# Performer attention, a merged expert layer and a routed expert layer: the place of the output's zeros, the queue of batch 1's stores, the engine of half the expert low parts, and the banks of the second kv half

## Chip, cores and metric

The kernel runs on one core of a Trainium2 chip. The metric is the device time of one execution in microseconds. Before the change the median of three runs is 358.18 us (357.52 to 359.08).

## What is computed

Three layers follow one another; all inputs and the output are float32.

```python
# 1. attention with random features, q and k: 2 batches x 8 heads x 576 tokens x 64
def phi(x):
    proj = np.einsum('bhsd,md->bhsm', x, omega)          # 128 features
    h = proj - np.sum(x * x, axis=-1, keepdims=True) / 2.0
    return np.exp(h - np.max(h, axis=-1, keepdims=True)) / np.sqrt(m)
q_p, k_p = phi(q * scale), phi(k * scale)
kv = np.einsum('bhsm,bhsd->bhmd', k_p, v)
num = np.einsum('bhsm,bhmd->bhsd', q_p, kv)
den = np.einsum('bhsm,bhm->bhs', q_p, np.sum(k_p, axis=2))[..., None] + 1e-06
x = num / den                                            # as 1152 tokens x 512
# 2. w1, w2: 512 x 1024, w3: 1024 x 1024, w_out: 1024 x 512
x = ((x @ w1) * (x @ w2) @ w3) @ w_out
# 3. 8 experts, each with 288 slots; a token goes to the expert of its largest logit
logits = x @ w_gate                                      # softmax of the chosen one: gate_w
h = np.maximum(np.einsum('ecd,edf->ecf', disp, e1), 0.0) # 512 -> 1024
y = np.einsum('ecf,efd->ecd', h, e2)                     # 1024 -> 512
out[i] = gate_w[i] * y[expert_idx[i], pos[i]]            # 0 for a token without a slot
```

## The kernel before

**Precision.** A float32 operand is split in a high part (a cast, on ScalarE) and a low part (operand less high part), and a product is made of three TensorE products: high by high, low by high, high by low. So each weight that arrives by DMA goes through a conversion before TensorE can use it. The weights w1, w2, w3 and w_out arrive as pairs of 32 bit words: VectorE puts the words together (lines 325 to 327 early, in `to_f32_task` later), ScalarE casts, and GpSimd subtracts (line 364). Expert weights arrive as float32: ScalarE casts (line 750) and VectorE subtracts (line 754), in two halves of 512 columns per piece.

**Stages.** First the features of k and q, in 18 units of 128 tokens (`phi_g`), the sums kv over the tokens of batch 0 and of batch 1 (`kv_add`; the accumulators are opened in PSUM by `kv_open`, closed by a copy to `kvz`), and the attention output x. PSUM has eight banks in three pools: `pa` with four, `pm` with two and `px` with two. Batch 0's kv lies in the two `pm` banks, batch 1's in the two `px` banks, which the projection of the features uses too. `KV_AT` names behind which unit which products of kv run.

Then a middle stage. It computes g = (x w1) * (x w2), transposed, in eight column blocks of 128 (f = 0 to 7) and four token chunks of 288 (`ab_mm`, line 433: 12 products of 128x288 each), and beside it W[f], the f-th 128 rows of w3 w_out (24 products of 128x512, line 472). W[f] is copied twice from PSUM by ScalarE and its low part is made on GpSimd (line 480). Its transpose (`u` pieces, line 492) and the product of that with w_gate (`v` pieces, line 500) lead to the logits, which are thus computed from g (`l` and `h` pieces, line 505), without x W.

Then routing and the expert stage. Each of the two batches has 576 tokens. g is transposed on VectorE and stored to a table in DRAM, `gd`, by `to_tokens`: for each batch two halves of four column blocks, and each half by four DMAs (line 410), on ScalarE's queue for the first half and SyncE's for the second. `route` finds expert and slot of each token (lines from 640 on), `gather` builds indices (`r_oh`, line 783) and fetches 288 rows by indirect DMA on GpSimd (line 806), `to_features` transposes them (`r_pt`), `product` multiplies by W (`r_x2p`, 96 products, with a high and a low part, x2, line 837), `hidden` by the expert's first matrix (`r_hp`, line 855) and `result_t` by its second (`r_yt`, line 893). `scatter` writes the rows to the output, which `zeroed` (lines 567 to 573) has filled with zeros by one DMA of 2304 KB. Round r0 holds the tokens of batch 0 for the expert most in demand at the head of the queue of experts, r1 those of batch 1; if more rounds were needed a loop at the end would run them.

**What sets the order.** TensorE's order is the order in which the program is written, and that is set by two strings: `PLAN` (middle stage) and `END` (rest). In `PLAN` a word is a piece: `aFB` the products of column block F for batch B, `WF` the products of W[F], `eFC` one token chunk, `uF`, `vF`, `lF`, `hF` as above, `cF` and `tF` the request for w1/w2 block F and for w3 block F, `z` the zeros. A request is put in a list (`push`); its load is issued on SyncE's queue as soon as one of the two buffers of its ring is free (`pump`). The stages of a conversion are issued one at a time by `tick()`, which the pieces call at their ends, and `need()` issues what is still missing. In `END` a letter is a step of a generator: `p` and `P` a part of `product` of r0 and r1, `h`/`H` of `hidden`, `s`/`S` of `result_t`, `t`/`T` of `to_features`, `K` and `R` logits and routing of batch 1, `F` its gather, `A` a block of g, and `.` is a `tick()`. `w`, `x` and `y` request expert weights; the letter `e` allows conversions of expert weights to begin. From the mark `|` in `PLAN` on, the order of ScalarE, VectorE, GpSimd and SyncE is fixed too, as it is emitted (`keep_order`): an instruction that waits holds all behind it on its engine.

The functions that the change touches:

## Time and profile before

| | us |
|---|---|
| median of three runs | 358.18 |
| lowest, highest | 357.52, 359.08 |
| the profiled execution | 358.03 |
| its span, first to last instruction | 356.1 |
| TensorE busy in the span | 332.1 |
| VectorE, ScalarE, GpSimd busy | 222.4, 146.8, 111.8 |

The profiled execution has its own time, 358.03 us; the span of its instructions is 1.9 us shorter, and all positions below are microseconds from the start of the span. The mean granted TensorE clock over the span is 0.972 of full speed. An engine's busy time says how much it worked; what it waited for is in brackets behind a row of the time line, with the idle time and the operation that ended it.

### The profile page before, as it was taken

What the parts mean: (1) busy time and instruction counts of PE and PEld (TensorE: products, weight loads), DVE (VectorE), ACT (ScalarE), POOL (GpSimd) and SP (SyncE); (2) the same over time, 40 slices, a digit from 0 to 9 for tenths busy, and PEclk for the clock granted to TensorE, in tenths of its full rate; (3) what the DMA queues carried; (4) which work ended last, traced back from release to release, by engine and by line L of the source; (5) the groups of instructions that cost most, each with busy time, mean ns of one, the idle gap of its engine ahead of it and who ended that gap; (6) DMA issues with size and microseconds to landing.
All of it is one profiled execution on the core that took longest, in us unless ns stands there. A gap on an engine that the chain in (4) does not pass through costs nothing. (4 is left out here: it accounts for less than half of the span.)

```text
span 356.1 us, 7072 instructions
## 1 busy us (share of the span) xinstructions
PE 332.1 (93%) x2771; PEld 306.5 (86%) x2771; DVE 222.4 (62%) x442; ACT 146.8 (41%) x347; POOL 111.8 (31%) x102
## 2 busy tenths in 40 slices
PE   7999799999998999989999959999996899999991
PEld 6899799999997988968898938899795799999991
DVE  4989999998997449455959230462764744743110
ACT  4998898634222432423343221222724145442100
POOL 4738610224352424634756521014000120120021
PEclk9999999999999999999999976999997899999998
DMA  7984202235457379923343630468595291510001
GB/s 262 395 311 149 62 2 61 61 120 140 159 151 259 123 109 204 244 65 118 115 124 120 249 135 2 86 49 245 166 183 147 82 291 56 202 44 2 1 24 50
DMA packets 25147, 47.76 MB, mean 134 GB/s; under 512 B 3116, under 2 KB 12460, under 8 KB 25110
## 3 DMA queue, kind: packets, MB, share of 16 engines
q1 hardware_dynamic: 19318, 41.36, 39.7%
q10 hardware_dynamic: 4736, 2.36, 4.1%
q0 software_dynamic: 1056, 3.54, 3.7%
q8 instruction: 24, 0.39, 0.5%
q14 instruction: 13, 0.11, 0.1%
HBM read 38.98 MB, written 8.27 MB: 133 GB/s over the span
## 5 line engine op out<-in xcount | busy, mean ns | idle before, releaser
L433 PE MATMUL ab<-xh,w_hl 128*128 128x288 f32 x512 | 110.4, 304 | 6.0 <-POOL w_hl L364 2.7
L433 PEld LDWEIGHTS ab<-xh,w_hl 128*128 128x128 f32 x512 | 85.4, 192 | 8.6 <-POOL w_hl L364 3.0
L433 PE MATMUL ab<-xl,w_hl 128*128 128x288 f32 x256 | 76.7, 300 | 0.0
L433 PEld LDWEIGHTS ab<-xl,w_hl 128*128 128x128 f32 x256 | 49.3, 193 | 0.0
L472 PE MATMUL W<-wo_hl,w_hl 128*128 128x512 f32 x192 | 46.6, 397 | 1.2 <-POOL w_hl L364 1.2
L472 PEld LDWEIGHTS W<-wo_hl,w_hl 128*128 128x128 f32 x192 | 35.4, 188 | 10.2 <-POOL w_hl L364 1.6
L364 POOL TENSOR_TENSOR w_hl<-w_f,w_hl 128x512 fp32r<-128x512 f32 x22 | 30.6, 1400 | 4.0 <-ACT w_hl L360 4.0
L405 DVE STREAM_TRANSPOSE gs<-g 128x576 f32<-128x576 f32 x16 | 19.6, 1223 | 18.8 <-POOL g L446 18.6
L350 DVE TENSOR_SCALAR w_f<-w_raw 128x512 uint32<-128x512 uint32 x22 | 15.0, 680 | 21.7 <-POOL w_hl L364 16.8
L834 PE MATMUL r_x2p<-r_xc,W 128*128 128x288 f32 x192 | 26.8, 298 | 0.2 <-DVE r_xc L823 0.2
L360 ACT CAST w_hl<-w_f 128x512 fp32r<-128x512 f32 x22 | 13.7, 624 | 31.3 <-DVE w_f L355 31.1
L834 PEld LDWEIGHTS r_x2p<-r_xc,W 128*128 128x128 f32 x192 | 25.8, 188 | 0.6 <-DVE r_xc L823 0.4
L437 ACT COPY a_sb<-ab 128x288 f32<-128x288 f32 x32 | 12.7, 398 | 29.3 <-PE ab L433 29.3
L869 POOL DMA_INDIRECT out<-r_yo,r_odx x6 | 6.1, 1024 | 57.7 <-DVE r_yo L868 48.7
L480 POOL TENSOR_TENSOR W<-W_raw,W 128x512 fp32r<-128x512 f32 x8 | 10.6, 1322 | 43.1 <-ACT u_all L501 27.7
L331 POOL TENSOR_TENSOR wo_hl<-wo_f,wo_hl 128x512 fp32r<-128x512 f32 x8 | 11.2, 1402 | 33.3 <-PE xT L276 16.9
L331 POOL TENSOR_TENSOR w_hl<-w_f,w_hl 128x512 fp32r<-128x512 f32 x10 | 14.2, 1418 | 22.5 <-ACT w_hl L330 19.9
L355 DVE SCALAR_TENSOR_TENSOR w_f<-w_raw,w_f 128x512 uint32<-128x512 uint32 x22 | 20.6, 935 | 0.6
L448 DVE TENSOR_TENSOR g<-a_sb,ab 128x288 f32<-128x288 f32 x20 | 8.9, 447 | 17.4 <-PE ab L433 17.4
L806 POOL DMA_INDIRECT r_xg<-gd,r_idx x6 | 5.7, 955 | 43.9 <-DVE r_odx L802 38.1
L446 POOL TENSOR_TENSOR g<-a_sb,b_sb 128x288 f32<-128x288 f32 x12 | 10.3, 858 | 25.2 <-ACT b_sb L445 25.2
L210 PE MATMUL pjq<-om_hl,q_hl 128*128 128x256 f32 x108 | 16.4, 293 | 0.0
(229 smaller groups left out, 691.6 us busy)
## 6 DMA issues: line engine op xcount, KB each, us to landing
w_raw<-in_w SPq DMA_DIRECT2D x32, 512.0 KB, 4.1
wo_raw<-in_wo SPq DMA_DIRECT2D x8, 512.0 KB, 3.6
v<-in_v SPq DMA_DIRECT2D x9, 260.0 KB, 5.3
k<-in_kT SPq DMA_DIRECT2D x9, 256.0 KB, 4.6
q<-in_qT SPq DMA_DIRECT2D x9, 256.0 KB, 6.5
gd<-gs ACTq DMA_DIRECT2D x8, 288.0 KB, 8.1
out<-zero SPq DMA_DIRECT2D x1, 2304.0 KB, 8.8
gd<-gs SPq DMA_DIRECT2D x8, 288.0 KB, 8.2
```

The costliest lines, as they stand in the source:

```text
L210: nc.tensor.matmul(out=ps[:, r * 256:(r + 1) * 256], lhsT=t[:, s, k * 128:(k + 1) * 128], rhs=om_hl[:, w], start=(n == 0), stop=(n == 2))
L331: nc.gpsimd.tensor_tensor(out=hl[1], in0=f.bitcast(F32), in1=hl[0].bitcast(F32), op=ALU.subtract)
L350: V.tensor_scalar(out=f, in0=r[:, :, 1], scalar1=3, scalar2=0x3FFFFFF8, op0=ALU.logical_shift_left, op1=ALU.bitwise_and)
L355: V.scalar_tensor_tensor(out=t["f"], in0=r[:, :, 0], scalar=29, in1=t["f"], op0=ALU.logical_shift_right, op1=ALU.bitwise_or)
L360: A.copy(out=h[:, 0], in_=t["f"].bitcast(F32))
L364: nc.gpsimd.tensor_tensor(out=h[1], in0=t["f"].bitcast(F32), in1=h[0].bitcast(F32), op=ALU.subtract)
L405: V.transpose(out=sts[b][:, :, :, f % GF], in_=g_t[f][:, b * S:(b + 1) * S].rearrange("p (j t) -> p j t", t=32))
L433: nc.tensor.matmul(out=p[:, :C], lhsT=w12[f][w][s][:, k, :], rhs=xhl[c][r][:, k], start=(n == 0), stop=(n == 11))
L437: A.copy(out=abp[f, c], in_=p[:, :C])
L472: nc.tensor.matmul(out=p, lhsT=w3_t[f, k // 4][s][:, k % 4, :], rhs=wo_t[k][r], start=(n == 0), stop=(n == 23))
L480: nc.gpsimd.tensor_tensor(out=w_t[f][:, 1], in0=raw, in1=w_t[f][:, 0].bitcast(F32), op=ALU.subtract)
L834: nc.tensor.matmul(out=p4[d][:, :C], lhsT=w_t[f][:, s, d * 128:(d + 1) * 128], rhs=xc[r][f // 4][:, f % 4], start=(f == 0 and (s, r) == (0 ...
```

## The change

Four edits, and new strings for the order:

- The second half of kv takes the two `pm` banks that the first half had, no longer the two `px` banks. The part of unit 4 that belongs to batch 1 is added at the next entry of `KV_AT` (with units 5 and 6).
- `PLAN`: the zeros (`z`) stand behind W7 and ahead of v6, where they stood ahead of a60; w1/w2 block 7 is requested ahead of W6 and block 6 ahead of W5, each earlier than before; W4 stands behind e42 and u3, where it stood ahead of them.
- Batch 1's stores of the second half of g go on ScalarE's queue, with a pause of one `tick()` between one and the next.
- The low part of the second half of each expert weight piece is made on GpSimd, where VectorE made both.
- `END`: expert conversions are allowed in four groups by the digits 1 to 4 (first matrix of r0, second matrix of r0, then those of r1), where `e` allowed all at once. Routing of batch 1 (`R`, `F`) is emitted earlier, r1's transposes begin behind the first quarter of r0's `result_t`, where they began behind the second, and alternate with the rest of it.

```diff
--- before.py
+++ after.py
@@ -48,14 +48,14 @@
 
 PLAN = (
     "g o7 a01 c2 o4 a10 o3 o0 a20 o2 a11 a21 c3 o1 o6 t0 o5 | t1 W0 a30 u0 t2 W1 v0 c4 a31 u1 "
-    "t3 W2 v1 a40 u2 t4 W3 v2 l0 l2 t5 W4 u3 c5 e42 v3 e43 u4 l1 t6 W5 v4 c6 a50 u5 t7 W6 v5 z "
-    "a60 c7 u6 W7 v6 l3 h5 e70 u7 h6 e71 v7 l4"
+    "t3 W2 v1 a40 u2 t4 W3 v2 l0 e42 t5 u3 W4 l2 v3 c5 e43 u4 l1 t6 c6 W5 v4 a50 u5 t7 c7 W6 v5 "
+    "a60 u6 W7 z v6 l3 h5 e70 u7 h6 e71 v7 l4"
 )
 
 
 
 
-END = "l<kAkrArfAAArfw>AAAA>AA<At.ttLttMt>e..K.p..K.p..p..Rp..p.p..Rh.h.RFh.Fh.h.h.xh.h..s..sTT..sTT..sTTss..yP..P..P..P..P..P..P.H.H.H.H.H.HHHSSSS"
+END = "l<kAkrArfAAArfw>AAAA>AA<At.ttLttMt>1K.p..K.p..Rp..p..p..RpF.2h..h.R.h..Fh..h..h..x3h..h..s.TT.sTT.sTT.s..ssy4P..P..P..P..P..P..P.H.H.H.H.H.HHHSSSS"
 
 
 @with_exitstack
@@ -109,7 +109,7 @@
 
 
     todo, active, out_of, done_of, LIM = [], [], {"wr": 0, "u": 0, "W": 0}, {}, {"wr": 2, "u": 2, "W": 2}
-    late, hold, leave = [False], [False], [False]
+    late, hold, leave = [False], [False], set()
 
     def push(key, ring, load, stages, first=False):
         t = {"key": key, "ring": ring, "load": load, "raw": None, "st": stages, "got": {}}
@@ -133,7 +133,7 @@
     def tick(n=1):
         for _ in range(0 if hold[0] else n):
             used = set()
-            while todo and (leave[0] or todo[0]["key"][0][0] != "e") and (todo[0]["ring"] is None or sum(t["ring"] is not None for t in active) < 2):
+            while todo and (todo[0]["key"][0][0] != "e" or todo[0]["key"][:2] in leave) and (todo[0]["ring"] is None or sum(t["ring"] is not None for t in active) < 2):
                 active.append(todo.pop(0))
             for t in list(active):
                 engs, fn, end = t["st"][0]
@@ -231,7 +231,7 @@
             nc.tensor.matmul(out=ps[:, 0:4 * (D + 1)], lhsT=zeros[:, 0:128], rhs=zeros, start=(k == 0), stop=False)
 
     def kv_open(b):
-        kvp[b] = [(pm, px)[b](f"kv{b}_{g}") for g in range(2)]
+        kvp[b] = [pm(f"kv{b}_{g}") for g in range(2)]
         for g in range(2):
             open_group(kvp[b][g], 1 if b else 9)
 
@@ -407,12 +407,12 @@
         def store(q):
             r0 = 1 + b * S
             c0 = f // GF * GF * 128 + q * GF * 32
-            (nc.scalar if f < GF else nc.sync).dma_start(out=gd[r0:r0 + S, c0:c0 + GF * 32].rearrange("(j p) c -> p j c", p=32),
+            (nc.sync if f >= GF and b == 0 else nc.scalar).dma_start(out=gd[r0:r0 + S, c0:c0 + GF * 32].rearrange("(j p) c -> p j c", p=32),
                                 in_=sts[b][32 * q:32 * q + 32].rearrange("p j c f -> p j (c f)"))
 
         st = [("V", turn, False)]
         if f % GF == GF - 1:
-            st += [("-", lambda _: None, False)] + [("S", lambda _, q=q: store(q), False) for q in range(4)]
+            st += [("-", lambda _: None, False)] + [x for q in range(4) for x in (("S", lambda _, q=q: store(q), False), ("-", lambda _: None, False))][:-1]
         if late[0]:
             push(("g", f, b), None, None, st, first=True)
         else:
@@ -517,7 +517,9 @@
         for i in KV_AT.get(n, ()):
             if i < 5:
                 kv_add(i, 0)
-            if i >= 4:
+            if i == 5:
+                kv_add(4, 1)
+            if i >= 5:
                 kv_add(i, 1)
         if n == 8:
             conv12(0)
@@ -751,13 +753,13 @@
 
         def lo(t, n):
             h, l, r = piece(t, n)
-            V.tensor_tensor(out=l, in0=r, in1=h.bitcast(F32), op=ALU.subtract)
+            (V, nc.gpsimd)[n].tensor_tensor(out=l, in0=r, in1=h.bitcast(F32), op=ALU.subtract)
 
         def both(t):
             lo(t, 0)
             hi(t, 1)
 
-        push(key, ring, load, [("A", lambda t: hi(t, 0), False), ("AV", both, False), ("V", lambda t: lo(t, 1), True)])
+        push(key, ring, load, [("A", lambda t: hi(t, 0), False), ("AV", both, False), ("P", lambda t: lo(t, 1), True)])
 
     def ask1(nm, ev):
         for q in range(4):
@@ -971,8 +973,8 @@
             logits(7, range(2, 4))
         elif p in "<>":
             hold[0] = p == "<"
-        elif p == "e":
-            leave[0] = True
+        elif p in "1234":
+            leave.add((("e1", "r0"), ("e2", "r0"), ("e1", "r1"), ("e2", "r1"))[int(p) - 1])
         elif p == "w":
 
             exd = const.tile([1, 1], I32, name="exd")
```

On GpSimd, the rows around W5 (L480; L364 are low parts of w1, w2 and w3, L446 products of g). Before:

```order
L446 TENSOR_TENSOR g4_2206<-a_sb_2429,b_sb_2449 128x288
L364 TENSOR_TENSOR w1_5_hl_2431<-w1_5_f_2389,w1_5_hl_2431 128x512
L364 TENSOR_TENSOR w2_5_hl_2465<-w2_5_f_2433,w2_5_hl_2465 128x512
L480 TENSOR_TENSOR W5_2508<-W5_raw_2509,W5_2508 128x512
L364 TENSOR_TENSOR w3_6_0_hl_2497<-w3_6_0_f_2481,w3_6_0_hl_2497 128x512
L446 TENSOR_TENSOR g5_2558<-a_sb_2538,b_sb_2559 128x288
L364 TENSOR_TENSOR w3_6_1_hl_2540<-w3_6_1_f_2499,w3_6_1_hl_2540 128x512
L446 TENSOR_TENSOR g5_2558<-a_sb_2577,b_sb_2597 128x288
```

After:

```order
L446 TENSOR_TENSOR g4_2205<-a_sb_2424,b_sb_2443 128x288
L364 TENSOR_TENSOR w1_5_hl_2458<-w1_5_f_2427,w1_5_hl_2458 128x512
L480 TENSOR_TENSOR W5_2501<-W5_raw_2502,W5_2501 128x512
L364 TENSOR_TENSOR w2_5_hl_2490<-w2_5_f_2472,w2_5_hl_2490 128x512
L446 TENSOR_TENSOR g5_2549<-a_sb_2529,b_sb_2550 128x288
L364 TENSOR_TENSOR w3_6_0_hl_2531<-w3_6_0_f_2492,w3_6_0_hl_2531 128x512
L446 TENSOR_TENSOR g5_2549<-a_sb_2570,b_sb_2590 128x288
L364 TENSOR_TENSOR w3_6_1_hl_2572<-w3_6_1_f_2533,w3_6_1_hl_2572 128x512
```

W5's row moved ahead of the low part of w2_5. The same holds at W6 and W7; at W7 the memset of the zeros stands in between too.

On SyncE's queue, the loads of the last blocks, the zeros, and batch 0's stores of g (gs4_0). Before:

```order
L344 DMA w3_7_0_raw_2609<-in_w3 128x1024
L344 DMA w3_7_1_raw_2611<-in_w3 128x1024
L571 DMA gd_100<-zero_2662 1x512 x2
L572 DMA gd_100<-zero_2662 1x1
L573 DMA out_0<-zero_2662 1152x1x512
L344 DMA w1_7_raw_2737<-in_w1 128x1024
L344 DMA w2_7_raw_2739<-in_w2 128x1024
L410 DMA gd_100<-gs4_0_2245 32x18x128 x4
```

After:

```order
L344 DMA w3_7_0_raw_2602<-in_w3 128x1024
L344 DMA w3_7_1_raw_2631<-in_w3 128x1024
L344 DMA w1_7_raw_2657<-in_w1 128x1024
L344 DMA w2_7_raw_2698<-in_w2 128x1024
L573 DMA gd_100<-zero_2785 1x512 x2
L574 DMA gd_100<-zero_2785 1x1
L575 DMA out_0<-zero_2785 1152x1x512
L410 DMA gd_100<-gs4_0_2244 32x18x128 x4
```

The loads of w1_7 and w2_7 moved ahead of the zeros, which stand directly ahead of the stores.

On ScalarE, r0's `product`: x2h is the copy of a finished part of it, e1 and e2 are casts of the expert's first and second matrix. Before:

```order
L750 CAST r0_e1_10h_3271<-r0_e1_1r_3089 128x512 x2
L750 CAST r0_e1_20h_3299<-r0_e1_2r_3091 128x512 x2
L750 CAST r0_e1_30h_3325<-r0_e1_3r_3093 128x512 x2
L837 CAST r0_x2h_3274<-r0_x2p0_3276 128x288
L750 CAST r0_e2_00h_3353<-r0_e2_0r_3269 128x512 x2
L654 ACTIVATE gex1_3360<-gsh1_3359 96x48
L837 CAST r0_x2h_3274<-r0_x2p1_3277 128x288
L750 CAST r0_e2_10h_3403<-r0_e2_1r_3297 128x512 x2
L837 CAST r0_x2h_3274<-r0_x2p2_3278 128x288
L750 CAST r0_e2_20h_3429<-r0_e2_2r_3323 128x512
L837 CAST r0_x2h_3274<-r0_x2p3_3279 128x288
```

After:

```order
L752 CAST r0_e1_20h_3315<-r0_e1_2r_3091 128x512 x2
L656 ACTIVATE gex1_3322<-gsh1_3321 96x48
L839 CAST r0_x2h_3265<-r0_x2p0_3267 128x288
L410 DMA gd_100<-gs4_1_2460 32x18x128
L752 CAST r0_e1_30h_3368<-r0_e1_3r_3093 128x512 x2
L839 CAST r0_x2h_3265<-r0_x2p1_3268 128x288
L410 DMA gd_100<-gs4_1_2460 32x18x128
L839 CAST r0_x2h_3265<-r0_x2p2_3269 128x288
L839 CAST r0_x2h_3265<-r0_x2p3_3270 128x288
L861 ACTIVATE r0_h00_3468<-r0_hp0_3472 128x288
L861 ACTIVATE r0_h00_3468<-r0_hp0_3473 128x288
L752 CAST r0_e2_00h_3502<-r0_e2_0r_3287 128x512 x2
```

All casts of the second matrix moved behind the four x2h copies and the first two copies of `hidden` (r0_h00), and two of batch 1's stores now stand between the copies.

## Rows read from the trace of the kernel before

**Rows 1.** Page, busy us of each engine, share of the span, instructions

```profile
PE 332.1 (93%) x2771; PEld 306.5 (86%) x2771; DVE 222.4 (62%) x442; ACT 146.8 (41%) x347; POOL 111.8 (31%) x102
```

**Rows 2.** Stretches: us, busy PE, PEld, DVE, ACT, POOL, granted clock, DMA, GB/s

```profile
35.60:44.50 8.90, 6.99 (x78) 6.29 (x79) 8.90 (x13) 7.53 (x18) 6.13 (x5) 1.00 0.21 62
...
213.60:222.50 8.90, 8.30 (x41) 7.64 (x42) 0.45 (x1) 0.98 (x2) 1.78 (x2) 0.64 0.01 2
...
267.00:275.90 8.90, 5.98 (x27) 4.99 (x26) 4.07 (x11) 4.24 (x10) 0.00 (x0) 0.74 0.57 150
```

**Rows 3.** Time line, TensorE's waits: start, us, instruction [idle before, what ended it]

```profile
37.33 1.09 PE L226 MATMUL tq<-ident,qp 128*128 128x128 f32 x8 [1.85 <-ACT kvz L252]
...
108.48 0.40 PE L433 MATMUL ab<-xh,w_hl 128*128 128x288 f32 x1 [0.93 <-ACT a_sb L437]
...
160.21 5.32 PE L472 MATMUL W<-wo_hl,w_hl 128*128 128x512 f32 x22 [1.17 <-POOL w_hl L364]
...
210.67 0.61 PE L433 MATMUL ab<-xh,w_hl 128*128 128x288 f32 x1 [2.23 <-ACT w_hl L360]
...
214.20 0.85 PE L433 MATMUL ab<-xh,w_hl 128*128 128x288 f32 x2 [2.68 <-POOL w_hl L364]
...
271.34 0.61 PE L855 MATMUL r_hp<-r_x2h,r_e_00h 128*128 128x288 f32 x1 [2.87 <-ACT r_x2h L837]
...
281.48 1.77 PE L789 MATMUL r_pi<-ids,r_oh 96*96 96x1 f16 x18 [1.57 <-DVE r_oh L783]
```

**Rows 4.** Time line, TensorE: products at full clock, and where slow stretches end

```profile
185.44 0.43 PE L433 MATMUL ab<-xh,w_hl 128*128 128x288 f32 x2
...
185.84 0.43 PE L433 MATMUL ab<-xh,w_hl 128*128 128x288 f32 x2
...
219.64 0.80 PE L492 MATMUL wT<-ident,W_raw 128*128 128x128 f32 x4
...
278.15 0.30 PE L855 MATMUL r_hp<-r_x2h,r_e_10h 128*128 128x288 f32 x1
```

**Rows 5.** Time line, VectorE beside GpSimd, and ScalarE's cast at 107.51

```profile
23.90 0.69 DVE L326 SCALAR_TENSOR_TENSOR w_f<-w_raw,w_f 128x512 uint32<-128x512 uint32 x1
...
29.29 1.66 DVE L326 SCALAR_TENSOR_TENSOR w_f<-w_raw,w_f 128x512 uint32<-128x512 uint32 x1
...
26.43 3.96 POOL L199 TENSOR_TENSOR q_hl<-q,q_hl 128x512 fp32r<-128x512 f32 x3
...
107.51 0.62 ACT L330 CAST w_hl<-w_f 128x512 fp32r<-128x512 f32 x1 [2.13 <-DVE w_f L327]
```

**Rows 6.** Time line around W5 on TensorE and GpSimd, and the zeros' memset

```profile
180.71 0.38 PE L433 MATMUL ab<-xh,w_hl 128*128 128x288 f32 x1
...
181.25 1.29 POOL L480 TENSOR_TENSOR W<-W_raw,W 128x512 fp32r<-128x512 f32 x1 [3.69 <-ACT u_all L501]
...
182.50 1.29 POOL L364 TENSOR_TENSOR w_hl<-w_f,w_hl 128x512 fp32r<-128x512 f32 x1
...
196.06 0.52 POOL L569 MEMSET zero<- 128x512 f32 x1
```

**Rows 7.** Time line: issue of r0's e2_1 load, and ScalarE's cast of it

```profile
257.92 1.15 SPq L737 DMA_DIRECT2D r_e_1r<-in_e  x1
...
269.85 1.14 ACT L750 CAST r_e_10h<-r_e_1r 128x512 fp32r<-128x512 f32 x2 [5.95 <-DMA r_e_1r<-in_e]
```

**Rows 8.** DMA issues view: count, KB each, median us from issue to landing

```profile
out<-zero SPq DMA_DIRECT2D x1, 2304.0 KB, 8.8
...
r_xg<-gd,r_idx POOLq DMA_INDIRECT x6, 9.3
```

**Rows 9.** Time line: issue of w1_7/w2_7 loads, stores and gather; first r_yt

```profile
198.23 1.95 SPq L344 DMA_DIRECT2D w_raw<-in_w  x2
...
226.29 3.83 SPq L410 DMA_DIRECT2D gd<-gs  x4
...
283.72 0.96 POOL L806 DMA_INDIRECT r_xg<-gd,r_idx  x1 [38.13 <-DVE r_odx L802]
...
289.59 0.43 PE L893 MATMUL r_yt<-r_h,r_e_00h 128*128 128x288 f32 x2
```

## Prediction

> **What bounds the kernel now.** I read the page's busy times first: TensorE is busy 332.1 of 356.1 us, the next engine, VectorE, 222.4 [rows 1]. So the time is TensorE's, and a change can win only by its waits (24 us in all) and by the stretches in which it computes slowly. The table by stretches shows both. From 35.60 to 44.50 VectorE works 8.90 of 8.90 us: there TensorE follows it. From 213.60 and from 267.00 VectorE is half idle or more, and the granted clock is 0.64 and 0.74 instead of 1.00 [rows 2]: part of each stretch ran at the lower of the two levels, 1.2 instead of 2.4 GHz. Then TensorE's own waits in order of time: seven that this change touches, 0.93 to 2.87 us [rows 3]. The two slow stretches lie right behind 2.23 + 2.68 us and behind 2.87 us of waiting; behind the 1.85 at 37.33 the clock stayed at 1.00 [rows 2, 3]. A long wait is so paid twice. To price the second payment I need one product at full clock: three take from 185.44 to 185.84, 0.133 us each [rows 4].
>
> The sum stands against the profiled execution, 358.03 us; the median of the three runs is 358.18, 0.15 more, and I let the two stand for one another. The tail behind the last expert product is not touched and costs what it did.
>
> **Part 1, kv banks.** The second half of kv takes the banks of the first, so the product at 37.33 no longer waits 1.85 us for kvz [rows 3]. At most that comes back: 1.85. But VectorE is full there [rows 2], and the middle stage starts with TensorE at 108.48 waiting for ScalarE's a_sb, behind a cast that waited 2.13 us for VectorE's words [rows 3, 5]. If VectorE ends no sooner, the 1.85 reappears there. What can move VectorE is the order of its work beside GpSimd's: the same operation took 0.69 us at 23.90 and 1.66 at 29.29, the second while a GpSimd subtraction ran [rows 5]. One such meeting more costs half a microsecond to one. I take -1.0, half of the wait; bounds -1.9 and +0.5.
>
> A rule speaks to that difference. The Trainium skill, "SBUF — State Buffer", section "Who interferes with whom", says that a VectorE instruction with two SBUF inputs contends with a GpSimd instruction that reads SBUF, and that the one issued first shuts the other out. By that rule a low part moved to GpSimd could stop VectorE for its whole length, which is the slower rival below; this trace agrees as far as one pair goes, 0.69 against 1.66.
>
> **Part 2, W4 behind e42.** W4 waits 1.17 us at 160.21 for its low part [rows 3]. The change puts 24 products (3.2 us by the price above) ahead of it: -1.2. Bounds -1.2 and 0.
>
> **Part 3, zeros behind W7.** The loads of the last w1 and w2 block are issued at 198.23, behind the write of zeros to the output (2304 KB, 8.8 us from issue to landing) [rows 8, 9]; their conversions come late, and TensorE waits 2.23 and 2.68 us for them [rows 3]. With the loads ahead of the zeros both go. From the start of the first wait, 210.67 - 2.23 = 208.44, to the next piece at 219.64 [rows 4], 11.2 us pass for 24 products, which at full clock are 3.2: -8.0 (4.9 of waiting, 3.1 of clock). Bounds: -8.0, and -4.9 if the clock stays low for another reason.
>
> **Part 4, release gates and route order in batch 0's product.** TensorE waits 2.87 us at 271.34 for ScalarE's x2h, because ScalarE stands at a cast of an expert weight that waits 5.95 us for its load, ended at 269.85 [rows 3, 7]. In the new order the x2h casts stand ahead of all e2 casts, so that load is no longer in their way. From 271.34 - 2.87 = 268.47 to 278.15 [rows 4] 9.7 us go for 23 products, 3.1 at full clock: -6.6 (2.87 and 3.7 of clock). Bounds -6.6 and 0 (the second rival). The wait for r_oh at 281.48 [rows 3] goes too, since routing is emitted earlier: -1.6, bounds -1.6 and 0.
>
> **Part 5, what the new order adds.** On GpSimd the low parts of w2_5, w2_6 and w2_7 now stand behind the subtraction of W5, W6 and W7 instead of ahead of it. What that costs is read at W5: column block 5's first product starts at 180.71; the subtraction runs from 181.25 for 1.29, and a low part is made in another 1.29, so from 182.50 to 183.79 [rows 6]. The third product of w2 needs it, twelve products and two more later: 180.71 + 14 x 0.133 = 182.6. That leaves 1.2 to 1.3 us of waiting, +1.3 at block 5 and +1.3 at block 6. At block 7 half a group of logit products more stands between, but also the zeros' memset of 0.52 [rows 6]: +0.6. Bounds per place: 0, if u's copies free GpSimd earlier, and 2.3, if an activation product stands ahead on GpSimd. Sum +3.2; by [rows 2, 3] waits of this size keep the clock.
>
> Batch 1's gather now has 24 result products ahead of its transposes where it had 48. In before it is issued at 283.72; with the median 9.3 us to land it is there at 293.0, and the products that start at 289.59 last 3.2 us, to 292.8 [rows 8, 9]: I take +0.4. Bounds 0 (a quicker landing) and 2.9 (two low parts of 1.29 now queue ahead of it on GpSimd, whose 16 new instructions are part of this change).
>
> **At nothing:** 16 low parts, 16 x 1.29 = 20.6 us, go from VectorE to GpSimd, which is busy 111.8 of 356.1 [rows 1, 6]; TensorE's 96 products per step cover them. If that cover is gone the casts behind them queue, as in the slower rival. Batch 1's stores cost ScalarE four issues with pauses between (SP's four of batch 0 took 3.83 us [rows 9]), beside TensorE's products.
>
> **The sum:** -1.0 - 1.2 - 8.0 - 6.6 - 1.6 + 3.2 + 0.4 = -14.8; 358.03 - 14.8 = **343.2 us**.
>
> **The rivals.** *A new wait halves the clock* (0.12). If a wait of part 5 passes about 2 us (1.85 kept the clock, 2.23 did not [rows 2, 3]), it costs 0.9 more and some 3.4 of clock (mean of the 3.1 and 3.7 above): 347.5 for one, 356.8 for all three (0.9 + 0.9 + 1.6 + 10.2 more). For it: GpSimd's order is fixed. Against it: my estimate is 1.3.
>
> *The load stays in the way* (0.10). The stores on ScalarE's queue still move bytes beside the expert loads; the load at 257.92 took 11.9 us [rows 7]. If it is as late against the new place of its cast, hidden's first copy waits as x2h did, and part 4's 6.6 stays: 349.8. This is the case that the change doesn't do what it says. The Trainium skill, "DMA: Bandwidth & Descriptors", section "Issuing engines are not separate DMA queues", has that the engine that starts a transfer gives it no transfer engines of its own; no row here tests it yet, and by it the move to ScalarE's queue buys nothing by itself.
>
> *The gather is late* (0.06): 2.9 us instead of 0.4, and the clock falls, 3.4: 349.1.
>
> *The zeros meet batch 0's stores* (0.04). The zeros are now issued about one microsecond after 208.44 of before's time (behind W7's casts, its subtraction of 1.3 and the memset of 0.5), land 8.8 later, near 218.3, and batch 0's stores stand behind them on SP at 226.29 - 8.0 = 218.3 [rows 8, 9]. If they wait for all of it, 8.8 and 3.4 of clock: 355.4.
>
> *Slower* (0.03): GpSimd's low parts lock VectorE out. One mechanism: each of the 16 shuts VectorE out for its 1.29 us, VectorE's own parts and the x2 and h low parts behind them come late, and TensorE follows: 343.2 + 20.6 = 363.8. It decides once more than 15 us of the 20.6 fall on TensorE's path. Against it: VectorE worked 4.07 of 8.90 us in the stretch [rows 2].
>
> *Nothing comes of it* (0.03): the waits are replaced by others of their size, 358.
>
> **How the numbers follow.** Forecast 0.62. The low end takes part 5 at nothing and part 1 at its best: 343.2 - 3.2 - 0.4 - 0.9 = 338.7. The high end, 350, takes in the late load, the late gather and one halved wait; outside lie all three halved (0.04 of the 0.12), the zeros, slower and nothing, 0.14. A measurement here tells about 0.5%, 1.8 us, from no change. Faster 0.94, same 0.03, slower 0.03.
>
> **What would show it.** Right: no wait before the products of column block 7 above 1 us and granted clock 1.00 there; x2h not waited for in batch 0's product and the clock near 1.00; waits of 1 to 1.5 us for w_hl from GpSimd in blocks 5 and 6; the wait at 108.48 grown by about 0.9, if the kv step is half lost. Wrong: a wait over 2 us followed by a half clock at a50, a60 or e70; ScalarE standing at an expert cast while hidden's first copy is due; r_pt of batch 1 waiting for the gather for over 1 us; low parts on VectorE longer than before.

## The result and the profile after

The changed kernel takes 344.53 us (median of four runs, 343.41 to 344.81) beside 358.53 us for the kernel before on the same chip: a ratio of 0.961 (95% interval 0.958 to 0.964), 14.0 us less. The forecast was 343.2 us, 14.8 less. The profiled execution took 343.41 us, its span is 341.5 us.

The busy times, as [rows 1] of before (engine, busy us, share of the span, instructions):

```profile
PE 325.2 (95%) x2771; PEld 300.8 (88%) x2771; DVE 218.8 (64%) x426; ACT 146.4 (43%) x347; POOL 134.2 (39%) x118
```

TensorE runs the same 2771 products in 325.2 us instead of 332.1, 6.9 us less, and is idle 341.5 - 325.2 = 16.3 us instead of 24.0, 7.7 less. So about half of the gain is clock and half is waiting: the two payments of the prediction, nearly even.

TensorE's waits on the time line, as [rows 3] (start, us, instruction, idle time before it and what ended it; behind the first feature units these are all over 0.3 us):

```profile
43.80 0.66 PE L226 MATMUL tq<-ident,qp 128*128 128x128 f32 x4 [1.38 <-ACT qpT L227]
...
107.53 0.40 PE L433 MATMUL ab<-xh,w_hl 128*128 128x288 f32 x1 [0.84 <-ACT a_sb L437]
...
181.74 0.53 PE L433 MATMUL ab<-xh,w_hl 128*128 128x288 f32 x2 [1.02 <-POOL w_hl L364]
...
196.81 0.53 PE L433 MATMUL ab<-xh,w_hl 128*128 128x288 f32 x2 [1.53 <-POOL w_hl L364]
...
212.71 0.53 PE L433 MATMUL ab<-xh,w_hl 128*128 128x288 f32 x2 [1.24 <-POOL w_hl L364]
...
282.90 1.22 PE L820 MATMUL r_pt<-ident,r_xg 96*128 96x96 f32 x8 [0.89 <-DVE r_xc L825]
```

The waits of 1.17 (W4), 2.23 and 2.68 (block 7), 2.87 (x2h) and 1.57 (r_oh) are gone. New are 1.02, 1.53 and 1.24 for the low parts of w2_5, w2_6 and w2_7, and 0.89 ahead of a transpose of batch 1. The stretches that answer to [rows 2] (us, then busy time and instructions of TensorE, its weight loads, VectorE, ScalarE, GpSimd; granted clock; DMA share; GB/s):

```profile
209.00:218.00 9.00, 7.76 (x56) 6.53 (x53) 0.46 (x1) 2.55 (x6) 2.98 (x3) 1.00 0.50 184
...
255.00:275.00 20.00, 20.00 (x168) 19.98 (x168) 14.04 (x53) 9.37 (x22) 8.09 (x7) 1.00 0.94 206
35.00:44.50 9.50, 8.01 (x87) 7.11 (x86) 9.50 (x18) 8.08 (x19) 9.38 (x7) 1.00 0.19 57
```

Block 7 and r0's product with `hidden` now run at a granted clock of 1.00, where they had 0.64 and 0.74. VectorE is still full while the kv sums are made, 9.50 of 9.50 us.

### The profile page after: what moved, and what is told of

Same layout as the page of the kernel before. It is cut to its first block, busy times and chain, and to the rows that moved or that the text cites. A ratio compares the mean times of both kernels' runs of the same rounds, so it can differ in the third digit from the quotient of the medians.

```text
span 341.5 us, 7108 instructions
## 1 busy us (share of the span) xinstructions
PE 325.2 (95%) x2771; PEld 300.8 (88%) x2771; DVE 218.8 (64%) x426; ACT 146.4 (43%) x347; POOL 134.2 (39%) x118
## 5 line engine op out<-in xcount | busy, mean ns | idle before, releaser
L433 PE MATMUL ab<-xh,w_hl 128*128 128x288 f32 x512 | 108.2, 299 | 4.8 <-POOL w_hl L364 3.8
L433 PEld LDWEIGHTS ab<-xh,w_hl 128*128 128x128 f32 x512 | 83.4, 188 | 8.1 <-POOL w_hl L364 4.5
L433 PE MATMUL ab<-xl,w_hl 128*128 128x288 f32 x256 | 75.5, 295 | 0.0
L433 PEld LDWEIGHTS ab<-xl,w_hl 128*128 128x128 f32 x256 | 48.1, 188 | 0.0
L350 DVE TENSOR_SCALAR w_f<-w_raw 128x512 uint32<-128x512 uint32 x22 | 17.4, 789 | 23.5 <-POOL w_hl L364 23.4
L364 POOL TENSOR_TENSOR w_hl<-w_f,w_hl 128x512 fp32r<-128x512 f32 x22 | 29.6, 1358 | 5.3 <-ACT w_hl L360 5.3
L480 POOL TENSOR_TENSOR W<-W_raw,W 128x512 fp32r<-128x512 f32 x8 | 10.8, 1355 | 37.3 <-ACT W L479 19.2
L331 POOL TENSOR_TENSOR w_hl<-w_f,w_hl 128x512 fp32r<-128x512 f32 x10 | 14.0, 1402 | 22.4 <-ACT w_hl L330 22.4
L446 POOL TENSOR_TENSOR g<-a_sb,b_sb 128x288 f32<-128x288 f32 x12 | 10.6, 879 | 25.0 <-ACT b_sb L445 25.0
L355 DVE SCALAR_TENSOR_TENSOR w_f<-w_raw,w_f 128x512 uint32<-128x512 uint32 x22 | 19.2, 872 | 0.6
L210 PE MATMUL pjq<-om_hl,q_hl 128*128 128x256 f32 x108 | 16.3, 293 | 0.0
L210 PE MATMUL pjk<-om_hl,k_hl 128*128 128x256 f32 x108 | 15.6, 297 | 0.6 <-ACT k_hl L198 0.5
```

The costliest lines, as they stand in the source:

```text
L210: nc.tensor.matmul(out=ps[:, r * 256:(r + 1) * 256], lhsT=t[:, s, k * 128:(k + 1) * 128], rhs=om_hl[:, w], start=(n == 0), stop=(n == 2))
L331: nc.gpsimd.tensor_tensor(out=hl[1], in0=f.bitcast(F32), in1=hl[0].bitcast(F32), op=ALU.subtract)
L350: V.tensor_scalar(out=f, in0=r[:, :, 1], scalar1=3, scalar2=0x3FFFFFF8, op0=ALU.logical_shift_left, op1=ALU.bitwise_and)
L355: V.scalar_tensor_tensor(out=t["f"], in0=r[:, :, 0], scalar=29, in1=t["f"], op0=ALU.logical_shift_right, op1=ALU.bitwise_or)
L364: nc.gpsimd.tensor_tensor(out=h[1], in0=t["f"].bitcast(F32), in1=h[0].bitcast(F32), op=ALU.subtract)
L433: nc.tensor.matmul(out=p[:, :C], lhsT=w12[f][w][s][:, k, :], rhs=xhl[c][r][:, k], start=(n == 0), stop=(n == 11))
```

## The experiments

Each kernel is the changed one with one edit, unless it says otherwise. As the first stage ends a microsecond or two earlier or later from one trace to the next (107.51 to 109.86), two traces are also compared from the wait at the start of the middle stage (107.53 in the changed kernel) to the end of the span: 341.5 - 107.53 = 234.0 us, and 356.1 - 108.48 = 247.6 before. This is called the rest of the span below. The runs were made on three chips; the kernel before, run beside each, took 357.95 or 358.44 us, against 358.53 beside the changed kernel. So a difference of under about 1 us from the changed kernel is read from the traces and not from the medians.

**The three new waits (w2_first).**

```diff
-        nc.gpsimd.tensor_tensor(out=w_t[f][:, 1], in0=raw, ...)      # in W(f)
+        def low(): nc.gpsimd.tensor_tensor(out=w_t[f][:, 1], in0=raw, ...)
+        if f < 5: low()
+        else: w_low.append(low)
...
         w12[f] = [k4(need(("1", f))), k4(need(("2", f)))]            # in ab_mm
+        while w_low: w_low.pop(0)()
```

> The changed kernel with one move on GpSimd: the subtraction of W5, W6 and W7 is emitted behind the low parts of w2_5, w2_6 and w2_7, where it stood ahead of them. Theory (the three new waits of 1.02, 1.53 and 1.24 us come from that order alone, since w2's cast was done before the subtraction ended): they go, but for about 0.2 at block 6, whose cast ends later; 344.5 - 3.6 = 340.9. Rival (GpSimd is simply full there, or VectorE's words are late): the waits only change their name, 344 to 345.

340.65 us (340.32 to 341.13), ratio to before 0.949 (0.944 to 0.954). At block 6 a wait of 0.33 is left, at blocks 5 and 7 none, and r0's first product (`r_x2p`) comes 3.5 us sooner, counted from the middle stage's first product. The trace of the changed kernel shows why nothing had to be paid for it (ScalarE and GpSimd ahead of block 5):

```profile
177.26 0.62 ACT L360 CAST w_hl<-w_f 128x512 fp32r<-128x512 f32 x1 [3.14 <-DVE w_f L355]
...
179.17 1.29 POOL L480 TENSOR_TENSOR W<-W_raw,W 128x512 fp32r<-128x512 f32 x1 [3.68 <-ACT u_all L501]
180.42 1.26 POOL L364 TENSOR_TENSOR w_hl<-w_f,w_hl 128x512 fp32r<-128x512 f32 x1
```

The cast of w2_5 was done at 177.88. GpSimd stood idle for 3.68 us until 179.17, because W5's subtraction was first in its order and not ready, and w2_5's low part was made behind it. So it was order, not load. Some of the gain is lost again behind it: the wait at r_pt is 1.28 us where it was 0.89, and the rest of the span is 231.0 us, 2.9 less than in the changed kernel.

**Where those waits came from (w4_back).**

```diff
-    "t3 W2 v1 a40 u2 t4 W3 v2 l0 e42 t5 u3 W4 l2 v3 c5 e43 ...
+    "t3 W2 v1 a40 u2 t4 W3 v2 l0 l2 t5 W4 u3 c5 e42 v3 e43 ...
```

> The changed kernel with W4 back ahead of u3 and e42, as before. Theory: the wait of 1.17 us for the low part of w3_4 comes back and nothing takes it up: 345.7. Rival (VectorE or GpSimd is later by as much further on, so the wait only moves): 344.5.

341.73 us (341.16 to 343.0), ratio to before 0.955 (0.951 to 0.958): not slower than the changed kernel but faster, against both theories. Its waits from the middle stage on:

```profile
160.00 5.32 PE L472 MATMUL W<-wo_hl,w_hl 128*128 128x512 f32 x22 [1.18 <-POOL w_hl L364]
...
211.07 0.53 PE L433 MATMUL ab<-xh,w_hl 128*128 128x288 f32 x2 [0.78 <-POOL w_hl L364]
...
281.26 1.21 PE L820 MATMUL r_pt<-ident,r_xg 96*128 96x96 f32 x8 [0.87 <-DVE r_xc L825]
```

The 1.18 at W4 came back as expected, but the waits at blocks 5 and 6 went and that at block 7 shrank. The stages of the conversions are issued by `tick()` in the order in which the pieces are written; with W4 at its old place GpSimd has both low parts of block 5 and of block 6 ahead of W5's and W6's subtraction again (a row of two L364 from 174.35 for 3.00 us, then L480 at 181.04), and the zeros' memset behind w2_7's low part.

The edit moves more than W4, though: the chunk l2 and the request for w1/w2 block 5 (c5) go back too, which the change had put later. The list of edits ahead of the prediction leaves these two out; its diff has them. No run separates them. The order in which the kernel emits GpSimd's rows, read with one of them moved at a time, says this: with W4 alone put back, only w2_5's low part stands ahead of W5's subtraction again; w2_6's and w2_7's places come back only with c5 as well; l2 plays no part. So a piece moved by 24 products and a request moved by one piece shifted the phase of the conversions behind them. Counted by waits, the two together took 1.17 away and added 1.02 + 1.53 + (1.24 - 0.78) = 3.01: a loss of 1.8. The rest of the span is 231.5 us, 2.5 less than in the changed kernel; the other 0.6 is not accounted for.

**The zeros (zeros_back, and zeros_alone on the kernel before).**

```diff
-    "... t7 c7 W6 v5 a60 u6 W7 z v6 l3 ..."     # zeros_back; zeros_alone makes
+    "... t7 W6 v5 z a60 c7 u6 W7 v6 l3 ..."     # the opposite move in before
```

> The changed kernel with the zeros back ahead of a60 and the request for w1/w2 block 7 back behind it, as before. Theory (the write of the zeros stood ahead of the last w1 and w2 loads, whose lateness cost 4.9 us of waiting and 3.1 of clock): 344.5 + 8.0 - 1.2 (the wait of 1.24 at block 7 that the new order has goes into it) = 351.3, with waits of 2 to 3 us at block 7 and a granted clock of about 0.6 behind them. Rival (the zeros now delay batch 0's stores by as much, which undoing gives back): 344 to 346.

> The kernel before with the zeros behind W7 and the request for w1/w2 block 7 ahead of W6, and no other edit (on GpSimd w2_7's low part so comes behind W7's subtraction). Theory (the term of 8.0, less a new wait of about 1 us at block 7): 358.3 - 8.0 + 1.0 = 351.3. Rival (undoing it in the changed kernel gave 3.9, so that is its size; something else of the new order made the rest): 354.4.

zeros_back: 348.42 us (347.86 to 349.0), 3.9 more than the changed kernel (4.9 in the rest of the span) instead of 6.8. zeros_alone: 352.81 us (349.54 to 353.94), ratio 0.984 (0.980 to 0.989), 5.6 less than before instead of 7. Of zeros_back, the waits:

```profile
197.91 0.82 PE L433 MATMUL ab<-xh,w_hl 128*128 128x288 f32 x2 [2.00 <-POOL w_hl L364]
...
214.84 0.69 PE L433 MATMUL ab<-xh,w_hl 128*128 128x288 f32 x2 [2.33 <-POOL w_hl L364]
```

and the stretches behind them:

```profile
195.00:204.00 9.00, 7.00 (x41) 6.77 (x41) 1.84 (x4) 2.24 (x5) 4.92 (x5) 0.81 0.70 265
...
214.00:219.00 5.00, 4.16 (x20) 4.16 (x21) 0.00 (x0) 0.40 (x1) 2.02 (x2) 0.66 0.02 3
```

The clock in them is 0.81 and 0.66. The load is as late as before, but TensorE comes to it later, having stood 1.02 and 2.00 us at blocks 5 and 6 and run at half clock behind the second. A late load costs only what TensorE would have been earlier. The wait at block 6 is a matter of its own: the zeros' memset (0.52 us at 196.12) stands ahead of w2_6's low part here, so the wait grew from 1.53 to 2.00, and the clock fell behind it. So this run doesn't price the late load alone; zeros_alone comes nearer. Of zeros_alone:

```profile
211.10 0.53 PE L433 MATMUL ab<-xh,w_hl 128*128 128x288 f32 x2 [0.78 <-POOL w_hl L364]
...
263.39 0.40 PE L855 MATMUL r_hp<-r_x2h,r_e_00h 128*128 128x288 f32 x1 [2.21 <-ACT r_x2h L837]
...
266.06 0.61 PE L855 MATMUL r_hp<-r_x2h,r_e_00h 128*128 128x288 f32 x1 [1.26 <-ACT r_x2h L837]
```

At block 7 4.91 us of waiting shrink to 0.78, which with 3.1 of clock is 7.2, nearly the term of the prediction; and r0's first product comes 7.1 us sooner than before, counted from the middle stage's first product. The expert stage then takes 1.0 back. The x2h stall is 3.47 us instead of 2.87, since the expert's loads do not come sooner by as much as TensorE does, and behind a wait of 1.77 for r_oh, at 273.67, the clock falls where it had not in before (last section). The rest of the span is 241.5, 6.1 less than before.

What made w2_7 late in before was its landing more than its issue. Its load is issued at 199.05 in before and at 198.70 in the changed kernel (w1_7's at 198.23 and 194.42), but VectorE begins the last step on its words at 211.06 in the one and at 206.98 in the other. In before, the first load behind the zeros took 9.8 us to land, beside a median of 4.1 for the loads of these weights.

**The order of the expert stage (end_back, gates_off, and end_alone on the kernel before).**

```diff
-END = "...Mt>1K.p..K.p..Rp..p..p..RpF.2h..h.R.h..Fh..h..h..x3h..h..s.TT.sTT.sTT.s..ssy4P..."
+END = "...Mt>1234..K.p..K.p..p..Rp..p.p..Rh.h.RFh.Fh.h.h.xh.h..s..sTT..sTT..sTTss..yP..."   # end_back
+END = "...Mt>1234K.p..K.p..Rp..p..p..RpF.h..h.R.h..Fh..h..h..xh..h..s.TT.sTT.sTT.s..ssyP..." # gates_off
```

> The changed kernel with the old order string of the expert stage (all four groups of expert conversions allowed at once, as before). Theory (ScalarE's order, casts of the second matrix between the x2h copies, and late routing made 8.2 us of the gain): 344.5 + 8.2 - 0.9 = 351.8, with a wait of TensorE for x2h of 2 to 3 us and a granted clock of about 0.7 behind it. Rival (the stores' move to ScalarE's queue freed the loads, and the order counts for little): 344.5 to 346.5, only the wait for r_oh of 1.6 comes back.

> The changed kernel with the new order string, but all four groups of expert conversions allowed at once; so r0's x2h copies stand behind casts of the second matrix on ScalarE again, and routing stays early. Theory (the casts' order is what counts): the copy of the third part waits for the load issued at 251.6, some 12 us, so until about 263: a wait of 3 us and a half clock, 344.5 + 6.6 = 351.1. Rival (the stores' new queue is what counts, the load lands in time): within 1 us of 344.5.

> The kernel before with the new order string of the expert stage and its release gates, and no other edit (batch 1's stores on SyncE's queue, all low parts on VectorE). Theory (the terms 6.6 and 1.6 are the order's alone): 358.3 - 8.2 = 350.1, no wait for x2h or r_oh. Rival (it takes the stores' move as well): 354 or more, with a cast on ScalarE waiting for a load ahead of x2h or hidden's first copy.

end_back 351.05 us (350.31 to 351.55), 6.5 more than the changed kernel; gates_off 350.16 us (349.49 to 350.83), 5.6 more; end_alone 348.26 us (347.29 to 349.34), ratio to before 0.973 (0.969 to 0.977), 10.2 less than before (358.44 beside it) and more than the 8.2 of the terms. In end_alone's trace the rest of the span is 11.0 us shorter than before: 0.8 of it lies ahead of r0's first product, where this edit changes nothing, and 9.7 between that and r0's first `result_t` product (`r_yt`). The sizes are those of the theory, but neither of the first two has the wait for x2h that it named. end_back, ScalarE at a cast, and a wait of TensorE:

```profile
258.89 1.14 ACT L752 CAST r_e_00h<-r_e_0r 128x512 fp32r<-128x512 f32 x2 [4.22 <-DMA r_e_0r<-in_e]
261.49 0.24 ACT L656 ACTIVATE gex<-gsh 96x48 f32<-96x48 f32 x1 [1.46 <-DVE goh L660]
...
272.62 2.22 PE L791 MATMUL r_pi<-ids,r_oh 96*96 96x1 f16 x18 [3.08 <-DVE r_oh L785]
```

and the two stretches from there:

```profile
270.00:275.00 5.00, 2.38 (x19) 2.13 (x20) 3.91 (x24) 0.00 (x0) 0.00 (x0) 0.67 0.26 79
275.00:280.00 5.00, 5.00 (x27) 5.00 (x27) 0.72 (x4) 0.52 (x2) 2.79 (x3) 0.65 1.00 358
```

gates_off, ScalarE and TensorE:

```profile
267.76 0.62 ACT L752 CAST r_e_20h<-r_e_2r 128x512 fp32r<-128x512 f32 x1 [5.88 <-DMA r_e_2r<-in_e]
268.29 0.71 ACT L861 ACTIVATE r_h<-r_hp 128x288 fp32r<-128x288 f32 x2
...
283.34 1.55 PE L820 MATMUL r_pt<-ident,r_xg 96*128 96x96 f32 x8 [3.77 <-DMA r_xg<-gd,r_idx]
```

In both ScalarE stands at a cast of the second matrix that waits for its load (4.22 and 5.88 us). What is held behind it differs: in end_back VectorE's low part of the same piece and with it routing, so r_oh is late; in gates_off hidden's copies, then VectorE's low parts of them, then the index and so the gather. (gates_off also has a wait of 0.99 us for x2's low part, at 264.96: there VectorE's routing stood ahead of it.) One cause in the main, and the place where TensorE feels it depends on what stands next in the fixed order. In end_alone ScalarE waits for a load only once in this stretch, 1.38 us at 275.17, and TensorE is busy 15.00 of 15.00 us at full clock:

```profile
264.00:279.00 15.00, 15.00 (x131) 14.98 (x130) 12.02 (x46) 7.28 (x16) 1.53 (x2) 1.00 0.86 187
```

So the term is the order's and the gates'; the stores' move is not needed for it.

**The stores' queue (stores_sp).**

```diff
-            (nc.sync if f >= GF and b == 0 else nc.scalar).dma_start(
+            (nc.sync if f >= GF else nc.scalar).dma_start(
```

> The changed kernel with batch 1's stores back on SyncE's queue. Theory (the x2h copies no longer stand behind the casts that wait for the loads, so their lateness is hidden): within 1 us of 344.5, with the loads of the second matrix landing later. Rival (the stores' queue is what freed the path): the first copies of hidden wait behind a cast, up to 344.5 + 6.6 = 351.1.

344.14 and 343.87 us in two runs, 347.07 and 348.05 in two others: median 345.61. The trace is of the run at 347.07, and shows why that one was longer (time line of ScalarE and TensorE):

```profile
283.29 0.62 ACT L752 CAST r_e_20h<-r_e_2r 128x512 fp32r<-128x512 f32 x1 [4.27 <-DMA r_e_2r<-in_e]
...
285.00 1.20 PE L820 MATMUL r_pt<-ident,r_xg 96*128 96x96 f32 x8 [1.94 <-DVE r_xc L825]
```

with the stretch behind it:

```profile
285.00:290.00 5.00, 5.00 (x28) 5.00 (x29) 3.13 (x6) 1.96 (x5) 1.29 (x1) 0.69 0.00 1
```

The wait of 0.89 at r_pt has grown to 1.94, and there the clock fell. In r0's product and `hidden`, where the prediction's second rival looked, nothing changed: r0's first `result_t` product (`r_yt`) comes 166.7 us behind the middle stage's first product in both traces. So the queue is worth nothing at the place that the prediction spoke of. That it lengthened the wait at r_pt is seen in one trace only; of the other three runs, the second long one among them, there is no trace.

**The low parts' engine (low_dve).**

```diff
-            (V, nc.gpsimd)[n].tensor_tensor(out=l, ...)
+            V.tensor_tensor(out=l, ...)
...
-        push(key, ring, load, [..., ("P", lambda t: lo(t, 1), True)])
+        push(key, ring, load, [..., ("V", lambda t: lo(t, 1), True)])
```

> The changed kernel with all low parts of the expert weights on VectorE, as before. Theory (they are off the path on either engine): within 1 us of 344.5. Rival (VectorE is what routing and the x2 and h low parts wait for, and the 16 parts of 0.68 us stand ahead of them): 1 to 4 us slower, with a later r_oh or r_x2l in the new trace.

343.17 us (342.31 to 343.5), ratio to before 0.960 (0.955 to 0.964): by the ratio it cannot be told from the changed kernel (0.961). The trace can tell: the rest of the span is 1.0 less, up to r0's first `r_yt` nothing differs (166.7 us behind the middle stage's first product in both), and the wait of 0.89 at r_pt is gone. The rows of the load of r1's e1_2 and of its cast, first in the changed kernel:

```profile
273.18 0.91 POOL L808 DMA_INDIRECT r_xg<-gd,r_idx  x1 [0.30 <-issue]
274.12 1.31 POOL L756 TENSOR_TENSOR r_e_21l<-r_e_2r,r_e_21h 128x512 fp32r<-128x512 f32 x1
...
275.45 0.33 SPq L739 DMA_DIRECT2D r_e_2r<-in_e  x1
...
281.19 0.62 ACT L752 CAST r_e_20h<-r_e_2r 128x512 fp32r<-128x512 f32 x1 [3.21 <-DMA r_e_2r<-in_e]
281.71 0.85 ACT L824 CAST r_xc<-r_pt 128x384 fp32r<-128x384 f32 x2
```

and in low_dve:

```profile
272.01 0.33 SPq L739 DMA_DIRECT2D r_e_2r<-in_e  x1
...
279.68 0.62 ACT L752 CAST r_e_20h<-r_e_2r 128x512 fp32r<-128x512 f32 x1 [1.69 <-DMA r_e_2r<-in_e]
```

On GpSimd the low part of r0's e2_21 stands behind the three issues of batch 1's gather, which end at 274.09. Its raw buffer is free at 275.43, the next load is issued at 275.45, and ScalarE's copy of xc stands behind the cast of that load. On VectorE the buffer is free 3.4 us sooner, and the cast starts 1.5 us sooner.

**The clock by itself (long_wait).**

```diff
+        for _ in range({5: 3, 6: 5}.get(f, 0)):          # in W(f), behind L480
+            nc.gpsimd.tensor_tensor(out=pad, in0=pad, in1=pad, op=ALU.subtract)
```

> The changed kernel with extra subtractions of a 128x128 scratch tile on GpSimd behind W5's (three) and W6's (five), ahead of the low parts that TensorE waits for; estimated from the 1.29 us of a 128x512 one, a quarter each: the waits of 1.02 and 1.53 us grow to about 2.0 and 3.1. They compute nothing that is used. Theory (a single wait well over 2 us is followed by a half clock, price some 3.4 us): clock 1.00 behind the first, about 0.7 behind the second, 344.5 + 1.0 + 1.6 + 3.4 = 350.5. Rival (it takes two such waits close together, as at 210 to 214 in the kernel before): clock 1.00 behind both, 347.1.

351.04 us (350.58 to 351.72), 6.5 more than the changed kernel. The eight subtractions took 1.36 and 2.31 us, more than estimated, so the waits grew to 2.33 and 3.35:

```profile
185.13 0.53 PE L433 MATMUL ab<-xh,w_hl 128*128 128x288 f32 x2 [2.33 <-POOL w_hl L364]
...
203.55 0.85 PE L433 MATMUL ab<-xh,w_hl 128*128 128x288 f32 x2 [3.35 <-POOL w_hl L364]
```

The stretches around them:

```profile
180.00:190.00 10.00, 7.67 (x48) 7.44 (x47) 3.09 (x6) 2.58 (x7) 5.71 (x7) 0.83 0.51 157
190.00:197.00 7.00, 7.00 (x38) 6.03 (x38) 5.64 (x8) 2.29 (x5) 3.32 (x3) 1.00 0.25 78
197.00:204.00 7.00, 3.65 (x26) 3.32 (x26) 2.22 (x6) 2.58 (x6) 4.54 (x7) 0.94 0.49 150
204.00:212.00 8.00, 8.00 (x47) 7.65 (x47) 3.63 (x6) 2.92 (x6) 3.81 (x4) 0.84 0.21 67
```

Behind each the clock falls, also behind the first, for which the expectation (at 2.0 us) had 1.00. The waits make 1.31 + 1.82 = 3.1 us of the 6.5. The clock makes 10 x 0.17 + 7 x 0.06 + 8 x 0.16 = 3.4, so 1.7 for each of the two, not 3.4. That a single wait is enough is shown; the price here is half of the one assumed.

**The kv banks (kv_back).**

```diff
-        kvp[b] = [pm(f"kv{b}_{g}") for g in range(2)]
+        kvp[b] = [(pm, px)[b](f"kv{b}_{g}") for g in range(2)]   # and kv_add(4, 1) at its old place
```

> The changed kernel with the second kv half back in the other pool's banks, as before. Theory (the wait for kvz was half hidden, since VectorE sets the end of that stage): 344.5 + 1.0 = 345.5, the middle stage's first wait ends near 108.5 where it ends at 107.5. Rival 1 (VectorE sets all of it): 344.5. Rival 2 (TensorE sets it): 344.5 + 1.85 = 346.4.

345.40 us (344.22 to 346.49), 0.9 more; alone this is within the spread. The position of the middle stage's first product says more, since twelve other traces show it too:

```profile
37.67 1.09 PE L226 MATMUL tq<-ident,qp 128*128 128x128 f32 x8 [1.73 <-ACT kvz L252]
...
108.96 0.40 PE L433 MATMUL ab<-xh,w_hl 128*128 128x288 f32 x1 [1.08 <-ACT a_sb L437]
```

The four kernels with the old banks have it at 108.30 to 109.86 (mean 108.90), the nine with the new banks that were otherwise alike up to there at 107.51 to 108.66 (mean 108.13): 0.8 us. (long_wait, at 109.62, has one memset more at its start and is left out.) The 109.86 is end_alone's, where the clock fell behind the wait for kvz (last section); without it the mean is 108.58 and the difference 0.45. The ranges overlap, so 0.4 to 0.8 is an estimate and not a proof. What is clear in every trace is the exchange: with the old banks a wait of 1.73 to 1.85 us for kvz near 38, with the new ones a wait of 1.38 for qpT near 44.

**Both mends together (best).** The edits of w2_first and low_dve.

> The kernel of run w2_first (low parts of w2_5, w2_6, w2_7 ahead of the subtractions of W5, W6, W7 on GpSimd) with all expert low parts on VectorE, as in low_dve. Theory (the two are in different stages and add): 340.65 - 1.35 = 339.3, with no wait of TensorE above 0.5 us between 110 us and the last product. Rival (the wait for r_xc that low_dve took away comes back, since this kernel arrives there 3.5 us sooner): 340.5.

340.18 us (339.77 to 341.83), ratio to before 0.951 (0.947 to 0.955), and so faster than both kernels; from w2_first's 340.65 it cannot be told. In the trace no wait over 0.41 us is left between 109 us and the last product, the 1.28 at r_pt in w2_first being gone, and the rest of the span is 229.5 against 231.0 in w2_first. The expected 339.3 was missed by 0.9; in this trace the middle stage started 0.6 later (108.66 against 108.06). The rival's time, 340.5, is as near as the theory's, but the wait that it named did not come back.

## Why the prediction was right, point by point

The total was right, 343.2 against 344.53, by a mechanism that was right (a long wait can be paid twice, in idle time and in clock) and by errors of single terms that nearly cancelled. That it came within 1.3 us is in part luck.

- **Part 1, kv banks, -1.0:** 0.4 to 0.8 by the position of the middle stage, 0.95 between the two traces. The size was about right, the way was not: the wait at the start of the middle stage did not grow by 0.9 (0.84 beside 0.93); much of the 1.85 went into a new wait of 1.38 us (43.80) where none over 0.3 us had stood.
- **Part 2, W4 behind e42, -1.2: the sign was wrong.** The wait of 1.17 went, but w4_back shows that this move, together with the later request for block 5, made most of the waits of part 5: a net loss of 1.8 by waits. The prediction read the new order of GpSimd correctly and priced it, but it put it down to no edit, and so called part 2 a gain without a cost.
- **Part 3, zeros, -8.0:** gone are 4.91 us of waiting, and the clock behind them is 1.00. Alone in the kernel before, the edit gave 7.1 up to r0's first product (the term less the new wait of 0.78) and 5.6 in all, as the expert stage took some back.
- **Part 4, release and routing, -8.2:** 10.2 alone in the kernel before (in the traces 9.7 between r0's first product and its first `r_yt`), 6.5 and 5.6 when undone. The ordering was the cause, as said; the row that stalls is not always x2h.
- **Part 5, +3.2 and +0.4:** 1.02 + 1.53 + 1.24 = 3.8 against 1.3 + 1.3 + 0.6. Block 7 was mis-sized: ScalarE's cast of W7 waited 0.84 us for the logit products that were to give cover, and W7's subtraction behind it with the low part. The gather itself landed in time; the wait at r_pt (0.89) was for ScalarE's xc.
- **"At nothing", the low parts: a cost of 1.0 (1.5 between w2_first and best).** TensorE's products did cover the subtractions. What they did not cover is the raw buffer, freed later since the subtraction stands behind the gather's issues: the prediction counted these two as queued, but the wrong way round, low parts ahead of the gather.
- **The rivals.** No wait of the middle or the expert stage passed 1.53 us, and behind all of them the clock stayed at 1.00. long_wait shows that a new long wait does bring the clock down and that the rival's price of 3.4 was twice too high there. Its bound of about 2 us was not safe: in two other traces the clock fell behind 1.75 and 1.77 (last section). The load did not stay in the way: between 212.71 and 282.90 TensorE has no wait over 0.3 us. The zeros did meet batch 0's stores (issued at 212.33 and 9.7 us in landing, the stores issued at 220.60 and 7.1 us in landing, beside 4.1 in before), but TensorE waited for neither. The Trainium skill, "DMA: Bandwidth & Descriptors", section "Issuing engines are not separate DMA queues", says that transfers share the same engines whichever engine starts them, so that a new queue buys none; stores_sp agrees as far as r0's product goes (166.7 us in both traces).

## What to carry to other kernels

Where an order is fixed and helper stages are issued between pieces, moving one piece or one request can move the phase of the conversions behind it: read the new order on each engine after the move, and charge what it shows to the edit that made it. In front of an instruction that waits for a load, put what the critical engine waits for next; the cheapest mends here (w2_first, the gates) only exchanged neighbours. And ask of an engine change not only who computes but when the buffer comes free, and what is queued ahead of the releasing instruction.

## What was not expected of the hardware

Low parts on both engines at once stretch each other far more than the pair of [rows 5]. In the changed kernel, VectorE and GpSimd:

```profile
275.86 3.85 DVE L756 TENSOR_TENSOR r_e_00l<-r_e_0r,r_e_00h 128x512 fp32r<-128x512 f32 x1
...
275.37 1.31 POOL L756 TENSOR_TENSOR r_e_31l<-r_e_3r,r_e_31h 128x512 fp32r<-128x512 f32 x1
276.63 1.29 POOL L756 TENSOR_TENSOR r_e_00l<-r_e_0r,r_e_00h 128x512 fp32r<-128x512 f32 x1
277.88 1.28 POOL L756 TENSOR_TENSOR r_e_10l<-r_e_1r,r_e_10h 128x512 fp32r<-128x512 f32 x1
```

A subtraction that takes 0.68 us alone took 3.85: it ended at 279.71, half a microsecond behind the last of GpSimd's row, whose parts took 1.3 us each, as alone. The Trainium skill, "SBUF — State Buffer", section "Who interferes with whom", says that the one that comes second is shut out; here it was shut out by several in a row. Near 250 us both lost: three on GpSimd took 1.74 to 1.79 us and one on VectorE 1.78. None of it fell on TensorE's path: behind the long one and one more low part VectorE stood idle for 1.98 us before its row at r_pt (L825). So the slower rival's mechanism is real, the prediction's sign for it (longer low parts on VectorE) came, and TensorE did not follow.

Of the clock, the traces show no sharp bound by the length of the wait. It stayed at 1.00 behind single waits of up to 1.57 us, and behind 1.73, 1.83 and 1.85 us for kvz. It fell behind 1.94, 2.00, 2.33, 3.08, 3.35 and 3.77 us, and also behind 1.75 for kvz in end_alone and 1.77 for r_oh in zeros_alone. First end_alone:

```profile
38.10 1.42 PE L226 MATMUL tq<-ident,qp 128*128 128x128 f32 x8 [1.75 <-ACT kvz L252]
...
38.00:43.00 5.00, 4.90 (x30) 4.91 (x31) 5.00 (x7) 3.64 (x9) 3.72 (x4) 0.66 0.08 7
```

and zeros_alone:

```profile
273.67 1.76 PE L789 MATMUL r_pi<-ids,r_oh 96*96 96x1 f16 x18 [1.77 <-DVE r_oh L783]
...
276.00:280.00 4.00, 4.00 (x21) 4.00 (x20) 0.46 (x1) 0.41 (x1) 2.69 (x3) 0.57 0.93 256
```

So between 1.7 and 1.9 us both happened, and what decides there stays open. What a fall costs is the length of a stretch times what its clock lacks: 5 x 0.34 = 1.7 us in end_alone and 4 x 0.43 = 1.7 in zeros_alone, as for each of the two in long_wait. Behind r_oh in end_back it is 5 x 0.33 + 5 x 0.35 = 3.4, twice that.
